# One maximum by GpSimd for all six stage 1 groups of batches 3 and 4

## The chip, the cores and the metric

The kernel runs on one core of one Trainium2 chip. The metric is the device time of one execution in microseconds (us). The core's engines run side by side, each through its own list of instructions in order: PE (TensorE, matmuls), DVE (VectorE), ACT (ScalarE), POOL (GpSimd) and SP (SyncE, which here only issues DMAs). They wait for each other through semaphores.

## What is computed

The input x has 4 batches of 12416 rows of 128 numbers. Two attention blocks follow each other, and a gated feed-forward layer:

```python
def mab(q, kv):
    s = scale * (q @ kv.transpose(0, 2, 1))
    s = s - s.max(-1, keepdims=True)
    a = np.exp(s)
    a /= a.sum(-1, keepdims=True) + 1e-09
    return a @ kv
h = mab(I, x)          # 32 learned rows look at all rows of a batch
attn = mab(x, h)       # every row of the batch looks at the 32 results

gate = 1.0 / (1.0 + np.exp(-(x @ w_gate)))    # x is attn here; d_ff is 1536
val = x @ w_val
out = (gate * val) @ w_out
```

Stage 1 is `h = mab(I, x)`: a softmax over all 12416 rows of a batch. Stage 2 is `mab(x, h)`: a softmax over 32 values in each row. The feed-forward layer takes nearly all of the time.

## The kernel before

**Steps and slots.** A batch's 97 chunks of 128 rows are six groups (0 to 5) of 16 chunks, and one chunk that is left over. The feed-forward layer works on blocks of four chunks, 24 blocks for a batch. A block takes eight steps, alternately of 1024 and 512 columns: PE fills a PSUM bank with gate values (`g_ps`) and one with values (`v_ps`), ACT takes tanh of the first (L1127), DVE multiplies (L1159, the product), and PE projects the product through `w_out` (L1200, into `acc_ps`). At the end of a block ACT copies the result to SBUF (L1219) and SP sends it out. A gate bank is filled two steps ahead, and is free only when tanh has read it. Two steps are one slot. `o` is the slot at which the layer begins a batch: 0, 96, 192, 288. The plan is a table, `at(slot, make, late)`: what stands at a slot is emitted after its first step, or with `late` after its second, and each engine does its work in that order. From slot 304 on the steps have another form, which the change does not touch.

**Beside the layer.** While the layer works on a batch, stage 1 of the next batch and stage 2 of both run in the gaps. Slots below are counted from `o`, so that slot 29 is `o + 29`; with `o` = 96 that is stage 1 of batch 3, with `o` = 192 that of batch 4. A block's output copy (L1219) falls late in slots 0, 4, 8 and so on.

**Stage 1, two ways.** (a) `plan_stage1`, for groups 2 and 3: PE scores the group (L246, 128x512 in PSUM), DVE takes the maximum of each row (L258), ACT takes the exponential from PSUM with that maximum as bias (L271), a DMA on SP's queue transposes it (L295), PE sums (L306), and ACT keeps the sum (L321). (b) `plan_shared`, for groups 0, 1, 4, 5 and the left-over chunk (`one`): ACT copies the scores to SBUF (`keep`, L368), into columns of the present batch's `xT` that stage 2 has done with (`place`). POOL raises a common maximum over them (`lift`, L385 to L389: subtract, clamp, add, for each group but the first; the last also folds the columns 512 to 256 to 128 and takes in `one`). DVE takes the maximum of the 128 columns left (`low`, L399), POOL adds the negative maximum to the scores (`lower`, L413), ACT takes the exponential (`weigh`, L417; L377 for `one`), then DMA (`turn`), sums (`part`) and one copy for two groups (`hold`, L431). `plan_combine` joins the partial sums of a batch; it weighs `NSH` of them.

**Stage 2 on POOL.** `plan_stage2` for a group: PE scores, ACT copies (L646), POOL takes the maximum and subtracts it (`lower`, L656 to L663), ACT takes the exponential (L672), POOL adds up and inverts (L680 to L686, `total`; L463 and on) and spreads the weights (L702, `spread`), SP transposes (L713). In this stretch POOL's list reads, by slots: `total` -1, `spread` 1, stage 2 `lower` 6, lifts 7, 11 and 15, `total` 19, `spread` 21, `low`'s lowerings 23 (groups 0, `one`, 1), stage 2 `lower` 24, an x load (L94, for `o` = 96 alone) 24, lowerings 29 (groups 4, 5). ACT's exponentials of stage 1 stand at 7, 11 (way a), 26, 27, 30, 42 and 46 (way b).

Of the kernel before, what the change touches and what calls it, by code (L numbers as in the profile page):

```python
# [17 lines left out]
P = 128  # L18
# [8 lines left out]
def kernel(  # L27
# [17 lines left out]
    NLO = NCH - NG * GC  # L45
# [10 lines left out]
    bp = ctx.enter_context(tc.tile_pool(name="bp", bufs=2))  # L56
    s1p = ctx.enter_context(tc.tile_pool(name="s1p", bufs=4))
# [26 lines left out]
    xn, xT = {}, {}  # L84
# [44 lines left out]
    for c, e in ((0, half0), (half0, n0)):  # L129
# [9 lines left out]
        out=identf[:],  # L139
        in_=identf[:],  # L140
# [42 lines left out]
    NS = len(groups)  # L183
    arrival = [0, NG] + list(range(1, NG))
    at_col = {s: p for p, s in enumerate(arrival)}
    EARLY = NS - 3
    SHARED = [(), (0, 1)] + [(0, 1, 4, 5)] * (B - 2)
    own = [[s for s in (arrival if b == 0 else [2, 3, 4, 5]) if s not in SHARED[b]] for b in range(B)]
    col_of = [{s: p for p, s in enumerate(o)} for o in own]
    PER = [1, 1] + [2] * (B - 2)  # L190
    NSH = [len(own[b]) + len(SHARED[b]) // PER[b] for b in range(B)]
    nml = const.tile([P, 1 + NS - EARLY], F32, tag="nml")
    l1l = const.tile([P, 1 + NS - EARLY], F32, tag="l1l")
    nm1s = [const.tile([P, NS], F32, name=f"nm1_{q}", tag=f"nm1_{q}") for q in range(2)]
# [28 lines left out]
    def at(slot, make, late=False):  # L223
        plan.setdefault((slot, late), []).append(make)


    def s1_place(b, s):
        return col_of[b][s]

# [8 lines left out]
        ng = min(4, n)  # L238
        return ng, n // ng, 32 * ng

    def s1_score_pe(b, s, tag):
        c0, n = groups[s]
        ng, w, R = s1_dims(s)
        s1 = ps.tile([P, 512], F32, tag=tag, name="s1_ps")
        for g in range(ng):
            nc.tensor.matmul(  # L246
                s1[32 * g : 32 * g + 32, 0 : w * P],
                indT[:],
                xT[b][:, c0 + g * w : c0 + (g + 1) * w, :].rearrange("c j t -> c (j t)"),
                start=True,  # L250
                stop=True,
            )
        return s1
# [39 lines left out]
    def s1_turn_dma(b, s, a1T):  # L293
        a1 = s1p.tile([P, 4, P], F16, tag="a1")
        nc.sync.dma_start(a1[:], a1T[:], transpose=True)  # L295
        return a1

    def s1_sum_pe(b, s, a1, hp, k0, k1, first=True, last=True):
        c0, n = groups[s]
        ng, w, R = s1_dims(s)  # L300
        for k in range(k0, min(k1, w)):
            for cols, src in ((slice(0, C), None), (slice(C, C + 1), ones16[:])):
                for g in range(ng):
                    if b == 0 and src is not None:
# [50 lines left out]
    def plan_shared(b, o, takes, tops, least, weighs, sums, holds, one, with_one):  # L355
        st = {}
        nm, hst, ns, no = nm1s[b % 2], hsts[b % 2], NSH[b], len(own[b])
        per = PER[b]

        def place(i):  # L360
            c = NLO + 8 * i
            return xT[b - 1][:, c : c + 8, :].rearrange("p j t -> p (j t)").bitcast(F32)

        def score(i):
            st["s1"] = s1_score_pe(b, SHARED[b][i], "m")

        def keep(i):
            nc.scalar.copy(out=place(i), in_=st["s1"][:])  # L368

        def score_one():  # L370
            s1 = s1_score_pe(b, NG, "m")
            st["one"] = s1p.tile([P, 512], F16, tag="a1T", name="one").bitcast(F32)[0:m, 0:P]
            nc.scalar.copy(out=st["one"], in_=s1[0:m, 0:P])

        def weigh_one():
            st["a1T"] = s1p.tile([P, 512], F16, tag="a1T", name="a1T")
            nc.scalar.activation(out=st["a1T"][0:m, 0:P], in_=st["one"], func=AF.Exp)  # L377

        def turn_one():
            st["a1"] = s1p.tile([P, 4, P], F16, tag="a1", name="a1")  # L380
            nc.sync.dma_start(st["a1"][:, 0, 0:m], st["a1T"][0:m, 0:P], transpose=True)

        def rise(near, far, w, R=P):
            top, r = place(4)[0:R, 0:w], place(5)[0:R, 0:w]
            nc.gpsimd.tensor_tensor(out=r, in0=far, in1=near, op=ALU.subtract)  # L385
            nc.gpsimd.tensor_scalar(
                out=r, in0=r, scalar1=BIG, scalar2=0.0, op0=ALU.min, op1=ALU.max
            )
            nc.gpsimd.tensor_tensor(out=top, in0=near, in1=r, op=ALU.add)  # L389

        def lift(i):
            rise(place(0) if i == 1 else place(4), place(i), 512)
            if i == len(SHARED[b]) - 1:
                for w in (256, 128):
                    rise(place(4)[:, 0:w], place(4)[:, w : 2 * w], w)
                rise(place(4)[0:m, 0:P], st["one"], P, m)

        def low():
            nc.vector.tensor_reduce(  # L399
                out=nm[:, no : no + 1],  # L400
                in_=place(4)[:, 0:128],
                axis=AX.X,
                op=ALU.max,
                negate=True,
            )
            lower(place(0), st["one"], place(1))
            for k in range(no + 1, ns):
                nc.gpsimd.tensor_copy(out=nm[:, k : k + 1], in_=nm[:, no : no + 1])

        def lower(*parts):  # L410
            for far in parts:
                near = nm[0 : far.shape[0], no : no + 1].to_broadcast(far.shape)
                nc.gpsimd.tensor_tensor(out=far, in0=far, in1=near, op=ALU.add)  # L413

        def weigh(i):
            st["a1T"] = s1p.tile([P, 512], F16, tag="a1T", name="a1T")
            nc.scalar.activation(out=st["a1T"][:], in_=place(i), func=AF.Exp)  # L417

        def turn(i):
            st[i] = s1_turn_dma(b, SHARED[b][i], st["a1T"])  # L420

        def part(i, k0, k1):
            if i % per == 0 and k0 == 0:
                st["hp"] = ps.tile([P, C + 1], F32, tag="m", name="hp_ps")
            if i == with_one and k0:
                s1_sum_pe(b, NG, st["a1"], st["hp"], 0, 1, False, False)
            s1_sum_pe(b, SHARED[b][i], st[i], st["hp"], k0, k1, i % per == 0, (i + 1) % per == 0)

        def hold(k):
            summed[b] += 1  # L430
            nc.scalar.copy(out=hst[:, no + k, :], in_=st["hp"][:])  # L431

        for i in range(len(SHARED[b])):
            at(o + takes[i], lambda i=i: score(i))
            at(o + takes[i], lambda i=i: keep(i), late=True)
            at(o + weighs[i], lambda i=i: weigh(i), late=True)
            at(o + weighs[i] + 1, lambda i=i: turn(i))
            at(o + sums[i], lambda i=i: part(i, 0, 2))
            at(o + sums[i] + 1, lambda i=i: part(i, 2, 4))
# [365 lines left out]
    a1T, a1 = {}, {}  # L805
# [46 lines left out]
    for j0, tag, copy in ((GC // 2, "v2", nc.scalar.copy), (GC - BC, "g1", nc.vector.tensor_copy)):  # L852
# [26 lines left out]
        out=top[:],  # L879
# [352 lines left out]
    for b in range(B):  # L1232
# [147 lines left out]
```

## Time and profile before

| what | value |
|---|---|
| three runs | 710.03, 710.17, 710.19 us; median 710.17 |
| the profiled execution | 710.04 us; its span, from first to last instruction, 708.3 us |
| DMA, mean over the span | 93 GB/s |
| products (L1159) of 1024 and of 512 columns, mean of one | 1.215 and 0.680 us |

The page gives each engine's busy time; the trace can be asked for instructions in order of time, for groups of them by line and shape, and for each engine's busy time in a stretch. Where instructions of one engine follow each other without a gap, the next one starts a little before the one ahead has ended, so that what an instruction costs its engine is read from start to start.

### The profile page before, as it was taken

How to read it: one execution, taken by the hardware profiler on the slowest of the kernel's cores; microseconds unless marked ns; L12 is line 12 of the kernel's file. 1: busy time of each engine (PE TensorE's matmuls, PEld its weight loads, DVE VectorE, ACT ScalarE, POOL GpSimd, SP SyncE). 2: the span in 40 equal slices, each digit the busy share in tenths (PEclk: the TensorE clock that was granted, in tenths of full speed). 3: DMA queues.
4: the chain of work that ended last, by engine and by line, in shares of the span. 5: the costliest groups of instructions: out<-in, count | busy, mean ns of one | idle time of the engine just before them, and what ended most of it. 6: DMA issues, size and time to landing. Idle time of an engine off the chain costs nothing.

```text
span 708.3 us, 21692 instructions
## 1 busy us (share of the span) xinstructions
PE 651.7 (92%) x8482; PEld 389.9 (55%) x8482; DVE 692.8 (98%) x806; ACT 680.2 (96%) x1115; POOL 458.3 (65%) x797
## 2 busy tenths in 40 slices
PE   7999899998999999999998989999899999999997
PEld 4555465555555555655555555555555555554555
DVE  4899999999999999999999999999999999999998
ACT  6799999999999999999999999999999999999997
POOL 4468865877558978668656896587757375482400
PEclk9999999999999999999999999999999999999999
DMA  9969854364583174156475141320322131221211
GB/s 214 181 123 192 139 133 93 76 121 86 114 161 80 57 127 101 51 125 118 92 139 124 54 77 53 69 76 31 78 63 74 47 60 48 59 76 46 63 46 46
DMA packets 118247, 65.80 MB, mean 93 GB/s; under 512 B 100320, under 2 KB 103296, under 8 KB 118144
## 3 DMA queue, kind: packets, MB, share of 16 engines
q1 hardware_dynamic: 113680, 50.93, 32.0%
q0 software_dynamic: 4272, 13.34, 10.7%
q8 instruction: 66, 1.08, 0.6%
q14 instruction: 37, 0.30, 0.2%
q10 hardware_dynamic: 192, 0.15, 0.1%
HBM read 27.80 MB, written 25.43 MB: 75 GB/s over the span
## 4 chain that ended last, share of the span: by engine, by line
DVE 35%; PE 29%; ACT 17%; issue 16%; DMA 2%; DVEq 0%; POOL 0%; POOLq 0%; ACTq 0%
DVE u L1159 33%; PE acc_ps L1200 14%; ACT t L1127 10%; PE v_ps L1064 10%; ACT xn L1106 5%; PE g_ps L1064 3%; DMA xn<-in_x_dram 2%; PE hp_ps L306 1%; ACT o L1219 1%; DVE nm L258 1%; DVEq L1159 0%; POOL xn L94 0%; ACT a1T L271 0%; ACT e L672 0%; ACT hwt L493 0%
## 5 line engine op out<-in xcount | busy, mean ns | idle before, releaser
L1159 DVE SCALAR_TENSOR_TENSOR u<-t,v_ps 128x512 f16<-128x512 f16 x609 | 528.3, 946 | 0.3 <-ACT t L1127 0.3
L1127 ACT ACTIVATE t<-g_ps 128x512 f16<-128x512 f32 x609 | 464.8, 821 | 10.5 <-ACT t L1127 4.0
L1200 PE MATMUL acc_ps<-wo,u 128*128 128x128 f16 x4644 | 333.8, 220 | 4.5 <-ACT o L1219 2.7
L1200 PEld LDWEIGHTS <-u 128*128 128x128 f16 x4644 | 261.9, 98 | 120.4 <-issue 117.8
L1064 PE MATMUL v_ps<-a2r,hwt 32*128 32x512 f16 (+1 forms) x1194 | 279.1, 372 | 40.5 <-DVE u L1159 39.1
L1064 PE MATMUL g_ps<-a2r,hwt 32*128 32x512 f16 (+1 forms) x1188 | 300.9, 376 | 1.0
L1064 PEld LDWEIGHTS <-hwt 32*128 32x128 f16 x2432 | 88.0, 91 | 150.8 <-issue 100.5
L1159 DVE SCALAR_TENSOR_TENSOR u<-xn,v_ps 128x1024 f16<-128x1024 f16 (+2 forms) x127 | 141.4, 1191 | 0.1
L1106 ACT ACTIVATE xn<-g_ps 128x512 f16<-128x512 f32 x249 | 126.7, 613 | 0.4
L702 POOL TENSOR_TENSOR a2n<-e,rs 128x2048 f16<-128x2048 f16 (+3 forms) x25 | 86.8, 3474 | 6.1 <-ACT t L1127 2.2
L680 POOL TENSOR_TENSOR sum<-e 128x256 f32<-128x256 f16 (+1 forms) x23 | 15.4, 670 | 109.7 <-ACT e L672 109.7
L463 POOL TENSOR_TENSOR near<-sme,minus 128x16 f32<-128x16 f32 (+1 forms) x22 | 65.2, 2965 | 1.6
L1219 ACT ACTIVATE o<-acc_ps 128x512 f32<-128x512 f32 x96 | 58.2, 606 | 0.9
L657 POOL TENSOR_SCALAR rise<-rise 128x256 f32<-128x256 f32 (+6 forms) x110 | 30.1, 273 | 9.6
L660 POOL TENSOR_TENSOR top<-top,rise 128x128 f32<-128x128 f32 (+3 forms) x88 | 28.3, 322 | 7.3
L680 POOL TENSOR_TENSOR sum<-sum 128x128 f32<-128x128 f32 (+3 forms) x92 | 28.3, 307 | 7.2
L656 POOL TENSOR_TENSOR rise<-top 128x128 f32<-128x128 f32 (+3 forms) x88 | 27.2, 309 | 6.9
L656 POOL TENSOR_TENSOR rise<-sc 128x256 f32<-128x256 f32 (+1 forms) x18 | 13.3, 738 | 21.0 <-ACT sc L646 20.9
L663 POOL TENSOR_TENSOR sc<-sc,top 128x512 f32<-128x512 f32 (+1 forms) x18 | 19.5, 1084 | 1.4
L612 PEld LDWEIGHTS <-xT 128*128 128x128 f16 x388 | 13.1, 96 | 11.7 <-issue 11.3
L94 POOL DMA_DIRECT2D xn<-in_x_dram x24 | 14.4, 607 | 6.5 <-DMA xn<-in_x_dram 5.6
L612 PE MATMUL s_ps<-hT,xT 128*128 128x32 f16 x388 | 18.1, 178 | 0.1
(173 smaller groups left out, 339.4 us busy)
## 6 DMA issues: line engine op xcount, KB each, us to landing
out_dram<-o SPq DMA_DIRECT2D x90, 256.0 KB, 2.2
xn<-in_x_dram POOLq DMA_DIRECT2D x19, 512.0 KB, 7.2
out_dram<-o SPq DMA_DIRECT2D x13, 128.0 KB, 1.7
xn<-in_x_dram POOLq DMA_DIRECT2D x3, 544.0 KB, 6.3
xT<-in_x_dram SPq DMA_DIRECT2D x1, 576.0 KB, 4.1
xT<-in_x_dram SPq DMA_DIRECT2D x1, 512.0 KB, 4.8
a2r<-a2n SPq DMA_TRANSPOSE x29, 4.4
xT<-xn SPq DMA_TRANSPOSE x27, 4.3
```

What stands on the lines that cost most here:

```text
L463: nc.gpsimd.tensor_tensor(out=near, in0=x, in1=minus, op=ALU.pow)
L612: nc.tensor.matmul(s2[:, j, :], xT[b][:, c + j, :], hT16[b][:], start=(j == 0), stop=whole and j == j1 - 1, skip_group_check=True,)
L656: nc.gpsimd.tensor_tensor(out=r, in0=far, in1=near, op=ALU.subtract)
L657: nc.gpsimd.tensor_scalar(out=r, in0=r, scalar1=BIG, scalar2=0.0, op0=ALU.min, op1=ALU.max)
L680: nc.gpsimd.tensor_tensor(out=d[:, 0:n, :], in0=src[:, :, 0:w], in1=src[:, :, w : 2 * w], op=ALU.add)
L702: eng.tensor_tensor(out=a2n[:, 0:n, :, :], in0=e.unsqueeze(2).to_broadcast((P, n, 4, m)), in1=rs.unsqueeze(2).unsqueeze(3).to_broadcast((P ...
L1064: st[what + "end"] = nc.tensor.matmul(to, hw[b][r : r + 32, j // 2, :], a2r[r : r + 32, o : o + nb, :].rearrange("p j t -> p (j t)"), star ...
L1106: nc.scalar.activation(out=ring_t(i, 1), in_=singles[i]["g"][:], func=AF.Tanh, scale=0.5)
L1127: st["tanh"] = nc.scalar.activation(out=st["t"][:, :, c:e], in_=st["g"][:, :, c:e], func=AF.Tanh, scale=0.5)
L1159: u = nc.vector.scalar_tensor_tensor(out=u16[:, :, c:e], in0=t16[:, :, c:e], scalar=1.0, in1=v32[:, :, c:e], op0=ALU.add, op1=ALU.mult,)
L1200: nc.tensor.matmul(acc[0][:, i, :], st["u"][:, n, ts(i, P)] if k < 2 else st["u1"][:, ts(i - st["kept"], P)], wo16[:, NI * (e % 2) + e // ...
L1219: nc.scalar.mul(out=o32[:], in_=acc[0][:], mul=0.5)
```

## The change

For batches 3 and 4 way (a) is dropped and all six groups go by way (b). The order among them is 2, 0, 3, 1, 4, 5. Groups 2 and 3 are scored and copied in two halves of 256 columns, and their exponentials are taken in four quarters of 128. Their scores lie in two tiles that are idle then (`"h"`, the other batch's `hst`, and `"x"`, the tile of `hx`); the common maximum and its scratch move to `home(2)` and `home(3)`. The partial sums are two instead of four.

By slots, before and after: copies -6, 2, 10, 14 become -7 and 1 (group 3, halves), -6 (0), -3 and -1 (group 2, halves), 2 (1), 10 (4), 14 (5); lifts 7, 11, 15 become 0, 2, 4, 11, 15; `low` 23 becomes 21 and lowers groups 0, `one`, 1; the later lowerings move from 29 (groups 4, 5) to 27 (groups 2, 3, 4, 5); exponentials become 26 (0), 29, 31, 33, 35 (group 2, quarters), 30 (1), 37, 39, 39, 41 (group 3, quarters), 42 (4), 46 (5); first sums become 31 (0), 33 (1), 40 (2), 44 (3), 48 (4), 51 (5); holds 45, 53 become 35, 53. The transposes of x of groups 2 and 3 move from -3 and 2 to -9 and -13. Stage 2's entries stay.

```diff
-    SHARED = [(), (0, 1)] + [(0, 1, 4, 5)] * (B - 2)
+    SHARED = [(), (0, 1)] + [(2, 0, 3, 1, 4, 5)] * (B - 2)
...
-    PER = [1, 1] + [2] * (B - 2)
-    NSH = [len(own[b]) + len(SHARED[b]) // PER[b] for b in range(B)]
+    SUMS = [(), ((0,), (1,))] + [((1, 3), (0, 2, 4, 5))] * (B - 2)
+    NSH = [len(own[b]) + len(SUMS[b]) for b in range(B)]
...
+    def at_half(time, make):
+        at(int(time // 1), make, late=time % 1 > 0)
...
+        homes = ('h', 0, 'x', 1, 4, 5) if b > 1 else (0, 1)
+        TOP, RISE = (2, 3) if b > 1 else (4, 5)
...
-        def keep(i):
-            nc.scalar.copy(out=place(i), in_=st["s1"][:])
+        def keep(i, part=slice(0, 4)):
+            cols = slice(part.start * P, part.stop * P)
+            nc.scalar.copy(out=place(i)[:, cols], in_=st["s1"][:, cols])
...
         def lift(i):
-            rise(place(0) if i == 1 else place(4), place(i), 512)
+            rise(place(0) if i == 1 else home(TOP), place(i), 512)
...
-            lower(place(0), st["one"], place(1))
+            soon = (1, 3) if b > 1 else (0, 1)
+            lower(place(soon[0]), st["one"], place(soon[1]))
...
-        def weigh(i):
-            st["a1T"] = s1p.tile([P, 512], F16, tag="a1T", name="a1T")
-            nc.scalar.activation(out=st["a1T"][:], in_=place(i), func=AF.Exp)
+        def weigh(i, part=slice(0, 4)):
+            cols = slice(part.start * P, part.stop * P)
+            if part.start == 0:
+                st["a1T", i] = s1p.tile([P, 512], F16, tag="a1T", name="a1T")
+            nc.scalar.activation(
+                out=st["a1T", i][:, cols], in_=place(i)[:, cols], func=AF.Exp
+            )
...
+        lowers = ((27, (0, 2, 4, 5)),) if b > 1 else ()
...
         at(o + least, low)
-        if len(SHARED[b]) > 2:
-            at(o + least + 6, lambda: lower(*[place(i) for i in range(2, len(SHARED[b]))]))
+        for slot, which in lowers:
+            at(o + slot, lambda which=which: lower(*[place(i) for i in which]))
...
-            parts = {2: (7, (16, 17, 17)), 3: (11, (18, 19, 19))}
-            turns = (-14, -5, -3, 2, 0, 8)
+            parts = {}
+            turns = (-14, -5, -9, -13, 0, 8)
             shared = (
-                (-6, 2, 10, 14),
-                (7, 11, 15),
-                23,
-                (26, 30, 42, 46),
-                (40, 42, 49, 51),
-                (45, 53),
+                ((-3, -1), (-6,), (-7.5, 0.5), (2,), (10,), (14,)),
+                (0, 2, 4, 11, 15),
+                21,
+                ((29, 31, 33, 35), (26,), (37, 38.5, 39, 41), (30,), (42,), (46,)),
+                (40, 31, 44, 33, 48, 51),
+                (35, 53),
                 (9, 27),
-                3,
+                5,
             )
```

In `lowers` and `soon` the numbers are places in the order above: 0 is group 2, 1 is group 0, 2 is group 3, 3 is group 1.

More of the change, by code (lines that the diff above doesn't have):

```diff
@@ L239, in s1_dims, with s1_score_pe @@
         return ng, n // ng, 32 * ng
-    def s1_score_pe(b, s, tag):
+    def s1_score_pe(b, s, tag, part=slice(0, 4)):
         c0, n = groups[s]
@@ L246, in s1_score_pe @@
             nc.tensor.matmul(
-                s1[32 * g : 32 * g + 32, 0 : w * P],
+                s1[32 * g : 32 * g + 32, part.start * P : min(part.stop, w) * P],
                 indT[:],
-                xT[b][:, c0 + g * w : c0 + (g + 1) * w, :].rearrange("c j t -> c (j t)"),
+                xT[b][:, c0 + g * w + part.start : c0 + g * w + min(part.stop, w), :].rearrange(
+                    "c j t -> c (j t)"
+                ),
                 start=True,
@@ L357, in plan_shared, with home, score @@
         nm, hst, ns, no = nm1s[b % 2], hsts[b % 2], NSH[b], len(own[b])
-        per = PER[b]
+        firsts, lasts = [g[0] for g in SUMS[b]], [g[-1] for g in SUMS[b]]
+        homes = ('h', 0, 'x', 1, 4, 5) if b > 1 else (0, 1)
+        TOP, RISE = (2, 3) if b > 1 else (4, 5)
         def place(i):
-            c = NLO + 8 * i
-            return xT[b - 1][:, c : c + 8, :].rearrange("p j t -> p (j t)").bitcast(F32)
-        def score(i):
-            st["s1"] = s1_score_pe(b, SHARED[b][i], "m")
-        def keep(i):
-            nc.scalar.copy(out=place(i), in_=st["s1"][:])
+            if homes[i] == "h":
+                return hsts[1 - b % 2].rearrange("p s c -> p (s c)")[:, 0:512]
+            if homes[i] == "x":
+                if "x" not in st:
+                    st["x"] = bp.tile([P, NS, C + 1], F32, tag="hx", name="far", bufs=1)
+                return st["x"].rearrange("p s c -> p (s c)")[:, 0:512]
+            return home(homes[i])
+        def home(k):
+            c = NLO + 8 * k
+            return xT[b - 1][:, c : c + 8, :].rearrange("p j t -> p (j t)").bitcast(F32)
+        def score(i, part=slice(0, 4)):
+            st["s1"] = s1_score_pe(b, SHARED[b][i], "m", part)
+        def keep(i, part=slice(0, 4)):
+            cols = slice(part.start * P, part.stop * P)
+            nc.scalar.copy(out=place(i)[:, cols], in_=st["s1"][:, cols])
         def score_one():
@@ L383, in rise @@
         def rise(near, far, w, R=P):
-            top, r = place(4)[0:R, 0:w], place(5)[0:R, 0:w]
+            top, r = home(TOP)[0:R, 0:w], home(RISE)[0:R, 0:w]
             nc.gpsimd.tensor_tensor(out=r, in0=far, in1=near, op=ALU.subtract)
@@ L391, in lift @@
         def lift(i):
-            rise(place(0) if i == 1 else place(4), place(i), 512)
+            rise(place(0) if i == 1 else home(TOP), place(i), 512)
             if i == len(SHARED[b]) - 1:
                 for w in (256, 128):
-                    rise(place(4)[:, 0:w], place(4)[:, w : 2 * w], w)
-                rise(place(4)[0:m, 0:P], st["one"], P, m)
+                    rise(home(TOP)[:, 0:w], home(TOP)[:, w : 2 * w], w)
+                rise(home(TOP)[0:m, 0:P], st["one"], P, m)
         def low():
@@ L400, in low @@
                 out=nm[:, no : no + 1],
-                in_=place(4)[:, 0:128],
+                in_=home(TOP)[:, 0:128],
                 axis=AX.X,
@@ L413, in lower, with pieces, add @@
                 nc.gpsimd.tensor_tensor(out=far, in0=far, in1=near, op=ALU.add)
-        def weigh(i):
-            st["a1T"] = s1p.tile([P, 512], F16, tag="a1T", name="a1T")
-            nc.scalar.activation(out=st["a1T"][:], in_=place(i), func=AF.Exp)
-        def turn(i):
-            st[i] = s1_turn_dma(b, SHARED[b][i], st["a1T"])
-        def part(i, k0, k1):
-            if i % per == 0 and k0 == 0:
+        def weigh(i, part=slice(0, 4)):
[5 more added lines that the diff above has]
+            )
+        def turn(i):
+            st[i] = s1_turn_dma(b, SHARED[b][i], st["a1T", i])
+        def pieces(slots):
+            cut = 4 // len(slots)
+            return [(slot, slice(k * cut, k * cut + cut)) for k, slot in enumerate(slots)]
+        def add(i, k0, k1):
+            if i in firsts and k0 == 0:
                 st["hp"] = ps.tile([P, C + 1], F32, tag="m", name="hp_ps")
@@ L426, in part @@
                 s1_sum_pe(b, NG, st["a1"], st["hp"], 0, 1, False, False)
-            s1_sum_pe(b, SHARED[b][i], st[i], st["hp"], k0, k1, i % per == 0, (i + 1) % per == 0)
+            s1_sum_pe(b, SHARED[b][i], st[i], st["hp"], k0, k1, i in firsts, i in lasts)
         def hold(k):
@@ L431, in hold @@
             nc.scalar.copy(out=hst[:, no + k, :], in_=st["hp"][:])
+        lowers = ((27, (0, 2, 4, 5)),) if b > 1 else ()
         for i in range(len(SHARED[b])):
[L434 to L439, printed above, removed]
+            for slot, part in pieces(takes[i]):
+                at_half(o + slot, lambda i=i, part=part: score(i, part))
+                at_half(o + slot + 0.5, lambda i=i, part=part: keep(i, part))
+            for slot, part in pieces(weighs[i]):
+                at_half(o + slot + 0.5, lambda i=i, part=part: weigh(i, part))
+            at(o + int(slot) + 1, lambda i=i: turn(i))
+            at(o + sums[i], lambda i=i: add(i, 0, 2))
+            at(o + sums[i] + 1, lambda i=i: add(i, 2, 4))
         at(o + one[0], score_one)
@@ L1263 @@
             turns = (5, 7, 17, 19, 22, 25, 9)
-            shared = (10, 14), (15,), 20, (26, 30), (33, 42), (34, 43), (13, 25), 0
+            shared = ((10,), (14,)), (15,), 20, ((26,), (30,)), (33, 42), (34, 43), (13, 25), 0
         else:
-            parts = {2: (7, (16, 17, 17)), 3: (11, (18, 19, 19))}
-            turns = (-14, -5, -3, 2, 0, 8)
+            parts = {}
+            turns = (-14, -5, -9, -13, 0, 8)
             shared = (
-                (-6, 2, 10, 14),
-                (7, 11, 15),
-                23,
-                (26, 30, 42, 46),
-                (40, 42, 49, 51),
-                (45, 53),
+                ((-3, -1), (-6,), (-7.5, 0.5), (2,), (10,), (14,)),
[4 more added lines that the diff above has]
+                (35, 53),
                 (9, 27),
-                3,
+                5,
             )
```

## The prediction

> **What bounds the kernel now.** I read the page first, then the busy time by stretches where stage 1 of batch 3 runs (slot 0 is at 201 us), then the timelines of ACT, DVE and POOL there.
>
> ```profile
> PE 651.7 (92%) x8482; PEld 389.9 (55%) x8482; DVE 692.8 (98%) x806; ACT 680.2 (96%) x1115; POOL 458.3 (65%) x797
> ```
>
> ```profile
> 200.00:220.00 20.00, 18.30 (x233) 11.12 (x231) 20.00 (x24) 19.71 (x31) 14.51 (x25) 1.00 0.72 155
> 220.00:240.00 20.00, 19.14 (x297) 11.95 (x294) 20.00 (x24) 19.70 (x32) 17.29 (x25) 1.00 0.15 49
> 240.00:260.00 20.00, 17.61 (x209) 10.26 (x207) 20.00 (x25) 19.70 (x31) 17.43 (x29) 1.00 0.51 88
> ```
>
> In the second view the columns after the length are PE, PEld, DVE, ACT, POOL, clock. DVE never rests: it is the bound, and ACT is close behind. POOL's 65% on the page hides that it is at 87% from 220 on.
>
> ```profile
> 201.02 0.60 ACT L1219 ACTIVATE o<-acc_ps 128x512 f32<-128x512 f32 x1
> ...
> 207.95 0.60 ACT L1219 ACTIVATE o<-acc_ps 128x512 f32<-128x512 f32 x1
> ...
> 215.53 0.61 ACT L1219 ACTIVATE o<-acc_ps 128x512 f32<-128x512 f32 x1
> ```
>
> ```profile
> 212.84 0.69 DVE L258 TENSOR_REDUCE nm<-s_ps 128x1 f32<-128x512 f32 x1
> ...
> 213.44 3.54 DVE L1159 SCALAR_TENSOR_TENSOR u<-t,v_ps 128x512 f16<-128x512 f16 x4
> ```
>
> Output copies end blocks of four slots. A block without a row maximum takes 6.93 us (201.02 to 207.95), 1.73 a slot; the one with L258 takes 7.58. From its start to the next product L258 costs DVE 0.60.
>
> **What is removed.** Two L258 in each of two batches: 4 x 0.60 = 2.4 us of the bound, if nothing else is late. The rest of this part asks what is late.
>
> **POOL's list.** This is the timeline of POOL for batch 3, first instructions of each task.
>
> ```profile
> 198.26 0.67 POOL L680 TENSOR_TENSOR sum<-e 128x256 f32<-128x256 f16 x1 [6.23 <-ACT e L672]
> ...
> 200.91 2.93 POOL L463 TENSOR_TENSOR near<-sme,minus 128x16 f32<-128x16 f32 x1
> ...
> 204.81 3.61 POOL L702 TENSOR_TENSOR a2n<-e,rs 128x2048 f16<-128x2048 f16 x1
> 212.08 0.73 POOL L656 TENSOR_TENSOR rise<-sc 128x256 f32<-128x256 f32 x1 [3.66 <-ACT sc L646]
> ...
> 219.71 1.27 POOL L385 TENSOR_TENSOR xT<-xT 128x512 f32<-128x512 f32 x1
> ...
> 223.10 1.27 POOL L385 TENSOR_TENSOR xT<-xT 128x512 f32<-128x512 f32 x1
> ...
> 227.32 1.27 POOL L385 TENSOR_TENSOR xT<-xT 128x512 f32<-128x512 f32 x1 [0.89 <-ACT xT L368]
> ...
> 235.59 0.65 POOL L680 TENSOR_TENSOR sum<-e 128x256 f32<-128x256 f16 x1
> ...
> 245.69 1.04 POOL L413 TENSOR_TENSOR xT<-xT,nm 128x512 f32<-128x512 f32 x1
> ...
> 248.18 0.72 POOL L656 TENSOR_TENSOR rise<-sc 128x256 f32<-128x256 f32 x1
> ...
> 255.77 0.67 POOL L94 DMA_DIRECT2D xn<-in_x_dram  x1
> 256.46 2.04 POOL L413 TENSOR_TENSOR xT<-xT,nm 128x512 f32<-128x512 f32 x2
> ```
>
> Start to start: `total` 2.65; `spread` 7.5 (200.91 to the end of L702, 208.42); stage 2 `lower` 7.63, later 7.59; a lift 3.39; the last lift with its folds 8.27; `total` and `spread` again 10.10; `low`'s lowerings 2.49; the load's issue 0.69; a lowering 1.02. The idle stretches are 3.66 and 0.89.
>
> After the change two lifts stand before stage 2's `lower`, one of them behind `total` and the others behind `spread`. That is five lifts for three, 2 x 3.39 = 6.78, and the idle time that they can fill is 4.55: POOL is 2.2 us later from there on, and has no rest. The list from 198.26: `total` to 200.91, lift 204.30, `spread` 211.8, two lifts 218.6, `lower` 226.2, lift 229.6, last lift 237.9, `total` and `spread` 248.0. Group 0 is lowered at 249.0, the others of `low` at 250.5. Then comes stage 2's `lower` of slot 24, to 258.1, the load to 258.8, and only then, from slot 27, group 2's lowering: **259.8**.
>
> **Who waits.** The timeline of ACT around slots 26 to 30:
>
> ```profile
> 247.58 0.63 ACT L417 ACTIVATE a1T<-xT 128x512 f16<-128x512 f32 x1
> 248.10 1.03 ACT L1127 ACTIVATE t<-g_ps 128x1024 f16<-128x1024 f32 x1
> 249.00 0.29 ACT L377 ACTIVATE a1T<-one 32x128 f16<-32x128 f32 x1
> 249.20 1.96 ACT L1127 ACTIVATE t<-g_ps 128x512 f16<-128x512 f32 x3
> 251.06 0.60 ACT L1219 ACTIVATE o<-acc_ps 128x512 f32<-128x512 f32 x1
> 251.53 3.09 ACT L1127 ACTIVATE t<-g_ps 128x1024 f16<-128x1024 f32 x4
> 254.51 0.63 ACT L417 ACTIVATE a1T<-xT 128x512 f16<-128x512 f32 x1
> ```
>
> ```profile
> 241.90 0.28 DVE L399 TENSOR_REDUCE nm<-xT 128x1 f32<-128x128 f32 x1
> ```
>
> Three waits appear, each a tighter form of the same lateness. (1) `low` moves from slot 23 (241.90) to 21: 241.9 - 3.46 - 1.2 = 237.2, but the folds end at 237.9, so DVE stands 0.7. (2) Group 0's exponential, slot 26, was at 247.58 and would be at 246.4 + 0.7 = 247.1; its lowering ends at 249.0: ACT stands 1.9. (3) Group 2's first quarter, late in slot 29: before, that place lies midway between 251.06 and 254.51, at 252.8. POOL is done at 259.8, **7.0 us after the old time**. Behind the waiting quarter on ACT stand the tanh's; behind them PE's gate fills and DVE's products. The third wait contains the other two and the 1.2 us gained, since after it the place in time is set by POOL alone.
>
> A quarter is not in the trace. Bounds: its nearest row, L377 of 32x128, takes 0.20 until tanh starts (249.00 to 249.20), and the full L417 takes 0.52; I take 0.20, and for DVE's distance behind ACT the same 0.2 (bounds 0 and 0.5), so they cancel.
>
> Batch 4 has the same list, from 366.03, without the load.
>
> ```profile
> 366.03 0.67 POOL L680 TENSOR_TENSOR sum<-e 128x256 f32<-128x256 f16 x1 [6.24 <-ACT e L672]
> ```
>
> ```profile
> 418.93 0.60 ACT L1219 ACTIVATE o<-acc_ps 128x512 f32<-128x512 f32 x1
> 419.40 3.10 ACT L1127 ACTIVATE t<-g_ps 128x1024 f16<-128x1024 f32 x4
> 422.38 0.63 ACT L417 ACTIVATE a1T<-xT 128x512 f16<-128x512 f32 x1
> ```
>
> Group 2 is lowered 61.5 - 0.7 = 60.8 after 366.03, at 426.9; slot 29 was at 420.7: **6.2 us**.
>
> **ACT's own load.** Four tanh take 2.76 (248.10 to 251.06, less 0.20), so two slots of 3.46 leave 0.70. Late in slots 37 to 41 lie four quarters and two copies of 0.47 (251.06 to 251.53): 1.74 for 1.40 of room. I take 0.2 a batch; bounds 0 (DVE's distance hides it) and 0.6, with quarters nearer to the full one. The half copies lie before slot 2, and what they cost is swallowed by wait 3. The two holds that go save ACT time where DVE is the bound: nothing. Scores in halves are more PE instructions before wait 3: nothing.
>
> The Trainium skill, "ScalarE: Activation LUTs", section "Rules for kernel authors", budgets about 0.3 us for an activation and 0.83 ns an element, an estimate of 0.41 for a quarter. By that the load term would be some 1 us a batch in place of 0.2; the row of L377 speaks for the smaller one.
>
> **SP and DMAs.** The transposes of x move to slots at which stage 1 still needs them 5 slots later or more: nothing. The distance from an exponential to its sum falls to 2.5 slots, 4.3 us, for group 1 (30 to 33) and group 3 (41 to 44).
>
> ```profile
> DMA to landing us min/median/max: 2.4/2.8/8.6
> ```
>
> That is L295, issue to landing. Exponential 0.6 and median 2.8 give 3.4: hidden, with under 1 us to spare. In batch 3 the loads of x, issued at 258.1 and after the lowerings at 262.9, lie around group 1's transpose; I take 0.6 there (bounds 0, and 8.6 + 0.6 - 4.3 = 4.9) and 0 in batch 4.
>
> **The sum.** 7.0 + 6.2 + 2 x 0.2 + 0.6 = 14.2 us on the profiled execution's 710.04: **724.2**. (The median, 710.17, is 0.13 above that execution.) A measurement of this kernel can tell about 0.2%, 1.4 us, from no change.
>
> **Rivals.** *The clock falls.* In wait 3 ACT stands from 254.4 (252.8 and the 1.6 of wait 2 over the old time) to 259.8, and PE, once its filled banks are full, for about 4.5 us of that. The trace shows one such rest, the end:
>
> ```profile
> 703.82 0.90 PE L1200 MATMUL acc_ps<-wo,u 128*128 128x128 f16 x13 [0.28 <-POOL u L1345]
> ```
>
> ```profile
> 704.00:709.00 5.00, 0.72 (x13) 0.54 (x10) 0.75 (x2) 0.38 (x1) 0.00 (x0) 0.95 0.15 52
> ```
>
> PE's last matmul ends near 704.7, and the granted clock, 1.00 in every stretch before, has 0.95 there: a fall some 4 us into the rest. PE at 92% of full speed cannot keep up at less. If the slow clock lasts as long as the rest, 4.5 us, half of it is lost: 2.2 a batch, 728.6 if both fall, 726.4 if one does. Chance 0.25: the rests are only a little longer than the one that showed the fall. The Trainium skill, "TensorE: Matmul & The Clock Gate", Part 1, has half speed after an idle window of about 3.4 us, and back after a busy one; by that 1.7 a fall, 727.6 for both. The trace agrees with the fall, and no run here shows the way back.
>
> *Only wait 2 bites.* If POOL takes the four lowerings ahead of the `lower` of slot 24, group 2 is done at 251.5 and wait 3 is gone; group 0's lowering at 249.0 against 247.58 still costs 1.4 a batch: 713.3 with ACT's load. Against it: POOL's rows follow the slots without exception (L656 of slot 24 before L413 of slot 29). Chance 0.05.
>
> *Faster: POOL is quicker than its rows.* The place is again slot 29, old time less the gain, 252.8 - 1.2 = 251.6. If POOL's 61.5 us from 198.26 took 53.3 or less, nothing would wait, and 2.4 less ACT's 0.4 remain: 708.0. It could be if POOL runs faster while DVE rests. Against it: POOL's L413 takes 1.04 and a lift 3.39 with DVE at 20.00 of 20, and DVE rests only after most of the chain has run. Chance 0.03.
>
> **How the numbers follow.** Forecast (both batches wait for POOL in slot 29, clock full): 0.67, 721.5 to 727 by the bounds of quarter, distance, load and transposes. Clock rival 0.25, up to 728.6; wait 2 alone 0.05; faster 0.03. The range 721 to 728.8 leaves out the last two and the ends of the others. Faster by over 0.2%: 0.03; within 0.2%: 0.02, from between the last two rivals; slower: 0.95.
>
> **What would show it.** Right: POOL without a rest from the `total` of slot -1 to the lowering of group 5; ACT's longest waits on POOL's L413 (its line will have moved), about 5.4 and 4.8 us at slot 29 and about 1.9 at slot 26; DVE idle by about 8 us in each of two stretches where it had none; no wait for stage 2's weights. Wrong: no such waits at a full DVE (then POOL's list isn't in the order that I read), PE's waits for transposes at slots 33 and 44 above 2 us, or a granted clock under 1.00 behind the waits (the rival).

## The result, and the profile after

| | median (lowest to highest), us | ratio to before, 95% interval |
|---|---|---|
| before, five runs | 710.05 (710.03 to 710.19) | |
| changed, five runs | 730.62 (730.03 to 732.06) | 1.0294 [1.0279, 1.0309] |
| forecast | 724.2 (721.0 to 728.8) | |

The change costs 20.6 us, 6.4 more than the 14.2 that were forecast. The execution profiled below took 732.06 us, the longest of the five.

The page of the changed kernel, its busy times and two of its rows in 40 slices:

```profile
PE 663.9 (91%) x8498; PEld 395.9 (54%) x8498; DVE 693.5 (95%) x802; ACT 683.4 (94%) x1131; POOL 472.6 (65%) x809
...
DVE  5899999999999859999999987999999999999998
...
PEclk9999999999999969999999998999999999999999
```

DVE has as much work as before (693.5 for 692.8 us) in a span that is 22 us longer: it waits. It does so in two places, slices 14 and 15 and slices 24 and 25, and right there the granted clock, which was full throughout before, falls.

The view of waits of the changed kernel says for what (waiting line, releaser, us in total, times, longest). ACT's exponentials (L417 before, now L437) wait for POOL's lowerings (L413, now L431):

```profile
ACT a1T L437 <- POOL hst L431: 9.2, 2, 4.7
...
ACT a1T L437 <- POOL xT L431: 3.7, 2, 1.9
```

```profile
DVE u L1188 <- PE g_ps L1093: 16.3, 15, 4.2
DVE u L1188 <- PE v_ps L1093: 3.8, 2, 1.9
```

ACT's waits are the forecast's wait 3 (`hst`, group 2) and wait 2 (`xT`, group 0), each once a batch. DVE, two steps behind, waits 20.1 us in all for PE's banks that come late for it; it had 15.5 us without work in the whole of before, and has 36.8 now.

POOL's timeline of the changed kernel around slot 27 of batch 3 (start, length):

```profile
198.56 0.67 POOL L709 TENSOR_TENSOR sum<-e 128x256 f32<-128x256 f16 x1 [6.54 <-ACT e L701]
...
248.09 1.04 POOL L431 TENSOR_TENSOR xT<-xT,nm 128x512 f32<-128x512 f32 x1
...
250.57 0.72 POOL L685 TENSOR_TENSOR rise<-sc 128x256 f32<-128x256 f32 x1
...
258.18 0.67 POOL L94 DMA_DIRECT2D xn<-in_x_dram  x1
258.88 1.05 POOL L431 TENSOR_TENSOR hst<-hst,nm 128x512 f32<-128x512 f32 x1
```

This is the list as it was read from the rows of before: `total` first (0.30 later than in before), group 0 lowered at 249.1 (forecast 249.0), then stage 2's `lower`, the load, and group 2 done at 259.93 (forecast 259.8). What ACT and DVE make of it:

```profile
249.16 0.63 ACT L437 ACTIVATE a1T<-xT 128x512 f16<-128x512 f32 x1 [1.87 <-POOL xT L431]
...
253.15 0.60 ACT L1248 ACTIVATE o<-acc_ps 128x512 f32<-128x512 f32 x1 [0.40 <-PE acc_ps L1229]
...
259.96 0.31 ACT L437 ACTIVATE a1T<-hst 128x128 f16<-128x128 f32 x1 [4.68 <-POOL hst L431]
260.17 1.50 ACT L1156 ACTIVATE t<-g_ps 128x1024 f16<-128x1024 f32 x2
...
267.01 0.60 ACT L1248 ACTIVATE o<-acc_ps 128x512 f32<-128x512 f32 x1 [0.72 <-PE acc_ps L1229]
```

```profile
238.03 0.29 DVE L416 TENSOR_REDUCE nm<-xT 128x1 f32<-128x128 f32 x1 [0.31 <-POOL xT L406]
...
251.18 1.82 DVE L1188 SCALAR_TENSOR_TENSOR u<-t,v_ps 128x1024 f16<-128x1024 f16 x2 [1.90 <-PE v_ps L1093]
...
261.87 1.22 DVE L1188 SCALAR_TENSOR_TENSOR u<-t,v_ps 128x1024 f16<-128x1024 f16 x1 [4.24 <-PE g_ps L1093]
```

All three waits are there: 0.31 for `low`, 1.87 for group 0, 4.68 for group 2. New are the two output copies (L1219, now L1248) that wait for PE, which no copy near these slots did before. Both fall in stretches of half clock. The granted clock in the records is constant over stretches of 3.41 us or whole multiples of it; cut at those places, the busy times of the changed kernel read (us, then PE, PEld, DVE, ACT, POOL busy, clock, DMA share, GB/s):

```profile
245.02:248.43 3.41, 3.01 (x39) 1.75 (x37) 3.41 (x5) 2.22 (x4) 3.41 (x2) 1.00 0.20 77
248.43:251.84 3.41, 1.51 (x15) 0.52 (x13) 1.51 (x3) 2.68 (x5) 3.26 (x6) 1.00 0.82 152
251.84:255.25 3.41, 3.41 (x30) 2.33 (x28) 2.70 (x4) 3.00 (x5) 2.81 (x7) 0.50 0.39 113
255.25:258.67 3.42, 1.89 (x23) 1.06 (x21) 2.10 (x3) 0.02 (x1) 2.92 (x8) 1.00 0.04 13
258.67:262.08 3.41, 0.85 (x18) 0.37 (x17) 0.21 (x1) 2.12 (x5) 3.38 (x5) 0.50 0.72 115
262.08:265.49 3.41, 3.41 (x44) 1.78 (x36) 2.37 (x3) 2.41 (x5) 1.36 (x2) 0.50 0.80 121
265.49:268.91 3.42, 3.02 (x38) 1.76 (x37) 2.28 (x3) 2.42 (x4) 0.00 (x0) 0.50 0.75 169
268.91:272.32 3.41, 3.41 (x41) 2.25 (x42) 2.12 (x3) 2.18 (x4) 0.00 (x0) 0.50 0.09 32
272.32:275.73 3.41, 3.07 (x46) 1.97 (x45) 2.93 (x4) 3.14 (x7) 2.19 (x7) 1.00 0.00 0
```

PE is busy for 1.51 of 3.41 us in the window of wait 2, and the next window runs at half clock; the same again after 1.89 of 3.42, at wait 3. The second fall lasts four windows, 13.65 us, though PE is busy for nearly all of the last three. In these DVE has 2.1 to 2.4 us of work in each 3.4: at half clock PE cannot feed it.

### The profile page after: what moved, and what is told of

It reads as the page before. It is cut to its first block, busy times and chain, and to the rows that moved or that the text cites. A ratio compares the mean times of both kernels' runs of the same rounds, so it can differ in the third digit from the quotient of the medians.

```text
span 730.3 us, 21759 instructions
## 1 busy us (share of the span) xinstructions
PE 663.9 (91%) x8498; PEld 395.9 (54%) x8498; DVE 693.5 (95%) x802; ACT 683.4 (94%) x1131; POOL 472.6 (65%) x809
## 4 chain that ended last, share of the span: by engine, by line
PE 29%; DVE 28%; issue 14%; ACT 13%; POOL 12%; DMA 4%; DVEq 0%; POOLq 0%; ACTq 0%
DVE u L1188 27%; PE acc_ps L1229 14%; PE v_ps L1093 9%; ACT t L1156 7%; ACT xn L1135 5%; PE g_ps L1093 3%; DMA xn<-in_x_dram 2%; POOL xT L406 2%; DMA a<-a1T 2%; POOL xT L402 1%; POOL top L689 1%; POOL rise L685 1%; ACT o L1248 1%; POOL a2n L731 1%; PE hp_ps L311 1%
## 5 line engine op out<-in xcount | busy, mean ns | idle before, releaser
L1229 PE MATMUL acc_ps<-wo,u 128*128 128x128 f16 x4644 | 338.6, 222 | 4.5 <-ACT o L1248 2.7
L1229 PEld LDWEIGHTS <-u 128*128 128x128 f16 x4644 | 266.6, 99 | 124.4 <-issue 121.2
L1093 PE MATMUL v_ps<-a2r,hwt 32*128 32x512 f16 (+1 forms) x1194 | 281.7, 376 | 39.7 <-DVE u L1188 36.8
L1248 ACT ACTIVATE o<-acc_ps 128x512 f32<-128x512 f32 x96 | 58.4, 608 | 3.0 <-PE acc_ps L1229 1.8
```

The costliest lines, as they stand in the source:

```text
L1093: st[what + "end"] = nc.tensor.matmul(to, hw[b][r : r + 32, j // 2, :], a2r[r : r + 32, o : o + nb, :].rearrange("p j t -> p (j t)"), star ...
L1229: nc.tensor.matmul(acc[0][:, i, :], st["u"][:, n, ts(i, P)] if k < 2 else st["u1"][:, ts(i - st["kept"], P)], wo16[:, NI * (e % 2) + e // ...
L1248: nc.scalar.mul(out=o32[:], in_=acc[0][:], mul=0.5)
```

## The experiments

Two theories stood against each other for the 6.4 us beyond the forecast. The first, A in the expectations, puts them down to the clock, which falls because PE rests in the waits. Its rivals put them down to ACT's additional pieces (halves and quarters) and to the transposes' shorter distance to their sums. A second question was whether POOL's lateness is the whole cause of the waits. The median of before, measured again beside these runs, was 709.88 (e1 to e4), 709.96 (e5 to e8) and 709.98 (e9, e10).

**e1_warm: PE kept busy in wait 3.** Added to the changed kernel are matmuls whose result nobody reads:

```diff
+        def warm(n):
+            w_ps = ps.tile([P, 512], F32, tag="m", name="warm_ps")
+            for _ in range(n):
+                nc.tensor.matmul(w_ps[:], wg16[:, 0:P], wg16[:, 0:512], start=True, stop=True)
+
+        if b:
+            at(o + 27, lambda: warm(8), late=True)
+            at(o + 30, lambda: warm(18), late=True)
```

> The changed kernel with matmuls that nobody reads (128x512, 8 late in slot 27 and 18 late in slot 30, batches 3 and 4), put where PE stands while ACT waits for POOL; everything else as it is. Theory A (the waits are POOL's lateness, 7.0 and 6.2 us, and what was lost behind them is PE's half clock): the waits of ACT stay as they are, the granted clock stays at 1.00, and some 4.3 us in batch 3 and 2.3 us in batch 4 come back: 724 us, 722.5 to 725. Rival B (behind the waits it is the late transposes and ACT's quarters that cost, and the clock only follows): the time stays near 730, within 1.5 us.

Measured: 730.57 us, 1.0284 [1.0268, 1.0300]. A's number missed and B's was met, but the cause that A names was not removed. The windows of this kernel's own clock stretches in batch 3:

```profile
255.95:259.36 3.41, 3.41 (x25) 1.85 (x24) 0.29 (x1) 0.00 (x0) 3.11 (x6) 1.00 0.09 13
259.36:262.77 3.41, 2.38 (x41) 1.36 (x39) 1.38 (x2) 3.08 (x6) 3.41 (x5) 1.00 0.91 157
262.77:266.18 3.41, 3.41 (x38) 1.77 (x35) 2.26 (x3) 2.62 (x6) 0.41 (x1) 0.50 0.82 124
```

PE still rested for 1.03 us at the end of the wait, and the clock still fell. In batch 4 wait 3 passed at full clock (slot 32 came only 6.3 us later), but then PE stood for the transposed exponentials of group 1 (1.03 us) and group 3 (1.46), and the clock fell behind the second. So the run settles nothing by its time. It led to e5, which closes these two holes, and to e6, its control.

**e5_warm_sums and e6_sums: the clock alone.** Both move the first sums of groups 1 and 3 a slot later, so that PE does not stand for the transposes; e5 keeps e1's matmuls too, with 23 in place of 18 for batch 3.

```diff
-                (40, 31, 44, 33, 48, 51),
+                (40, 31, 45, 34, 48, 51),
...
+            at(o + 27, lambda: warm(8), late=True)
+            at(o + 30, lambda b=b: warm(23 if b == 1 else 18), late=True)
```

> As e1_warm, with 23 matmuls in slot 30 of batch 3 (18 left 1.0 us of rest there, 18 in batch 4 none over 0.5), and the first sums of groups 1 and 3 one slot later (34 and 45 for 33 and 44), so that PE doesn't wait for their transposes. Theory A (7.0 and 6.2 us from POOL's list, some 0.5 a batch from ACT's load, the rest from the clock and from transposes): clock 1.00 throughout, 723.5 to 725.5. Rival B (something else costs the 6 us behind the waits): 728 or more with the clock at 1.00.

> The changed kernel with the first sums of groups 1 and 3 one slot later alone. PE's waits for transposes in it come to 1.6 us: if they are on the path and nothing hides them, 729.0; if the half clock is what PE stands on there and the transposes are hidden by it, 730.6, no change; theory A says between the two, 729 to 730.6, with the same falls of the clock.

Measured: e5 725.51 us, 1.0217 [1.0204, 1.0231]; e6 730.00, 1.0275 [1.0260, 1.0291]. Span and mean granted clock of the profiled executions, e5's and then e6's:

```profile
core 0: 723.4 us, clock 0.999
```

```profile
core 0: 728.2 us, clock 0.979
```

e5 does more work on PE than e6, waits as long for POOL (its longest wait of an exponential is even longer, 5.3 us), and is 4.5 us faster: that is the clock, for two batches, in each of which it fell twice in e6. It is A's forecast at its upper edge, where B had 728 or more. Output copies on ACT's timeline measure the rest. Of before, slots 32 and 48 of batch 3 and slot 32 of batch 4:

```profile
257.98 0.61 ACT L1219 ACTIVATE o<-acc_ps 128x512 f32<-128x512 f32 x1
...
285.68 0.60 ACT L1219 ACTIVATE o<-acc_ps 128x512 f32<-128x512 f32 x1
...
425.85 0.60 ACT L1219 ACTIVATE o<-acc_ps 128x512 f32<-128x512 f32 x1
```

Of e5, slots 32 to 48 of batch 3 and slot 32 of batch 4:

```profile
264.99 0.64 ACT L1248 ACTIVATE o<-acc_ps 128x512 f32<-128x512 f32 x1
272.10 0.69 ACT L1248 ACTIVATE o<-acc_ps 128x512 f32<-128x512 f32 x1
279.27 0.70 ACT L1248 ACTIVATE o<-acc_ps 128x512 f32<-128x512 f32 x1
286.33 0.60 ACT L1248 ACTIVATE o<-acc_ps 128x512 f32<-128x512 f32 x1
293.81 0.60 ACT L1248 ACTIVATE o<-acc_ps 128x512 f32<-128x512 f32 x1
...
440.41 0.63 ACT L1248 ACTIVATE o<-acc_ps 128x512 f32<-128x512 f32 x1
```

Slot 32 is 7.0 us late (264.99 for 257.98): POOL's wait of batch 3. At slot 48 it is 8.1 (293.81 for 285.68): 1.1 us came after the wait, in blocks of 7.1 to 7.5 us where before had 6.9. Slot 32 of batch 4 is 14.6 late (440.41 for 425.85): 6.4 more, POOL's wait of batch 4. So of e5's 15.5 us the waits are 13.4, and 2.1 are left for the pieces. Of these the copies show 1.1 and 0.6 (behind slot 32 of batch 4); 0.4 no copy shows, since the profiled executions lie only 15.2 us apart.

**e2_early and e3_both: POOL's list in time.** e2 lowers groups 2 and 3 together with groups 0 and 1, ahead of stage 2's `lower`. e3 also lets the copies of groups 2 and 3 trade places, so that the first lift goes to slot -3, into POOL's 6.5 us of rest ahead of `total`.

```diff
-            soon = (1, 3) if b > 1 else (0, 1)
-            lower(place(soon[0]), st["one"], place(soon[1]))
+            soon = (1, 3, 0, 2) if b > 1 else (0, 1)
+            lower(place(soon[0]), st["one"], *[place(i) for i in soon[1:]])
...
-        lowers = ((27, (0, 2, 4, 5)),) if b > 1 else ()
+        lowers = ((27, (4, 5)),) if b > 1 else ()
```

The second step, in e3 alone:

```diff
-            turns = (-14, -5, -9, -13, 0, 8)
+            turns = (-14, -5, -13, -9, 0, 8)
             shared = (
-                ((-3, -1), (-6,), (-7.5, 0.5), (2,), (10,), (14,)),
-                (0, 2, 4, 11, 15),
+                ((-7.5, -4.5), (-6,), (-1, 0.5), (2,), (10,), (14,)),
+                (-3, 2, 4, 11, 15),
```

> The changed kernel with groups 2 and 3 lowered together with 0, the left-over chunk and 1 in low (slot 21), ahead of stage 2's lower of slot 24; groups 4 and 5 stay at 27. Theory A (wait 3 is POOL's order): the wait at slot 29 goes, the wait at slot 26 stays at 1.9 us; each batch then stands 1.6 us behind the kernel before at slot 26 and loses up to 0.9 more to ACT's quarters: 713 to 715, up to 717 if the clock still falls at slot 26. Rival B (transposes and quarters cost the rest of the 20 us): no less than 720.

> As e2_early, and the copies of groups 2 and 3 trade places (group 2 in halves at slots -7 and -4, group 3 at -1 and 1; their transposes of x at -13 and -9), so that the first lift can stand at slot -3, in POOL's rest of 6.2 us ahead of total. Theory A: POOL's list is then 3.4 us earlier, no engine waits for it, and what is left is 2.4 us of row maxima gained, less what halves and quarters cost ACT, 0.3 to 1.5 us a batch: 708.3 to 710.6, middle 709.4. Rival B: 715 or more. If the maxima were not worth 2.4 us, above 711.

Measured: e2 718.66 us, 1.0123 [1.0109, 1.0137]; e3 711.60, 1.0024 [1.0015, 1.0033]. Both lie above what was expected: e2 above the 717 allowed for with a fall, though below the 720 of its rival, and e3 above 710.6. e2 is the prediction's rival "only wait 2 bites" made real, and is 5 us above the 713.3 priced there: one wait of 1.9 us a batch is left, and it lowers the clock by itself. Two windows of e2:

```profile
248.54:251.95 3.41, 1.53 (x15) 0.56 (x13) 1.53 (x3) 2.88 (x5) 3.41 (x5) 1.00 0.88 165
251.95:255.36 3.41, 3.41 (x32) 2.21 (x31) 2.77 (x4) 3.01 (x6) 3.07 (x7) 0.50 0.34 106
```

e3 has neither wait nor fall (clock 1.00 until the end) and is 7.1 us faster than e2. Of that 3.7 are ACT's waits for POOL and 0.5 DVE's (`low`); the other 2.9, some 3 us, are put down to two falls, of 3.41 us in batch 3 and 6.83 in batch 4. That is a difference of kernels whose copies also stand at other places. With POOL in time 19 of the 20.6 us are gone. What e3 still loses, 1.7 us, is neither a wait for POOL nor clock.

**e4_idle_lifts and e10_four_idle: POOL's lateness alone.** These go from the kernel before, with DVE's maxima where they were, and add lifts on an idle tile whose values nobody uses: two a batch in e4, four in e10.

```diff
+        def idle_lift(q):
+            scr = hsts[q].rearrange("p s c -> p (s c)")[:, 0:512]
+            nc.gpsimd.tensor_tensor(out=scr, in0=scr, in1=scr, op=ALU.subtract)
+            nc.gpsimd.tensor_scalar(
+                out=scr, in0=scr, scalar1=BIG, scalar2=0.0, op0=ALU.min, op1=ALU.max
+            )
+            nc.gpsimd.tensor_tensor(out=scr, in0=scr, in1=scr, op=ALU.add)
+
+        if b:
+            for slot in (0, 2):
+                at(o + slot, lambda q=b % 2: idle_lift(q))
```

In e10 the slots are `(0, 2, 3, 4)`.

> The kernel before, with two lifts more on POOL at slots 0 and 2 of batches 3 and 4, over a tile that is idle then and whose values nobody uses. Theory A: POOL is 2.2 us later at low's lowerings, group 0's exponential at slot 26 waits about 1.4 us in each batch, nothing else waits: 712.5 to 713, up to 715 if the clock falls there. Rival (POOL has room, the change was late for another reason): 710.0, no wait.

> The kernel before with four idle lifts (slots 0, 2, 3, 4) instead of e4_idle_lifts' two, which were 2.83 us each and moved POOL's list by 1.1. Theory A: 11.3 us of work into 4.55 of rest puts group 0's lowering 6.8 us later, ACT stands 5.9 us at slot 26 in each batch; with a PE that is idle for most of a 3.4 us window the clock falls, which cost 2.2 a batch in the changed kernel: 722 to 726, and half clock in the trace behind both waits though nothing of stage 1 was changed. Rival (the falls come of the changed kernel's own PE work): clock 1.00, 721.5 to 722.

Measured: e4 710.58 us, 1.0009 [1.0000, 1.0019]; e10 725.50, 1.0219 [1.0205, 1.0233]. e4's expectation missed on its price for a lift. POOL's timeline of e4:

```profile
200.68 1.04 POOL L1282 TENSOR_TENSOR hst<-hst 128x512 f32<-128x512 f32 x1
201.80 0.61 POOL L1283 TENSOR_SCALAR hst<-hst 128x512 f32<-128x512 f32 x1
202.50 1.04 POOL L1286 TENSOR_TENSOR hst<-hst 128x512 f32<-128x512 f32 x1
```

With the same tile for both operands a pass takes 1.04 us, for 1.27 with two tiles, and the lift 2.8 for 3.39. Two of them fill 5.7 us, POOL's idle 4.55 takes most, and the 1.1 left is about the reserve that POOL had ahead of ACT (0.85: in before group 0's lowering ended at 246.73, and ACT took it up at 247.58). The one wait of ACT for it that the view of waits lists in e4 is 0.2 us, and the clock does not fall. So e4 shows how little POOL had to spare, and e10 what follows beyond it. ACT in e10 and the clock around it:

```profile
253.68 0.63 ACT L417 ACTIVATE a1T<-xT 128x512 f16<-128x512 f32 x1 [5.32 <-POOL xT L413]
```

```profile
249.50:252.91 3.41, 0.71 (x9) 0.31 (x7) 0.86 (x2) 0.00 (x0) 3.41 (x2) 1.00 0.02 5
252.91:256.32 3.41, 0.99 (x4) 0.10 (x3) 0.40 (x1) 2.56 (x5) 3.31 (x6) 0.50 0.81 149
256.32:259.74 3.42, 3.42 (x28) 2.25 (x28) 2.65 (x4) 2.94 (x5) 2.80 (x7) 0.50 0.31 80
```

The waits for POOL in e10, ACT's and those of DVE, whose maximum in `low` (L399) now comes late too:

```profile
ACT a1T L417 <- POOL xT L413: 10.5, 2, 5.3
```

```profile
DVE nm L399 <- POOL xT L389: 1.3, 2, 0.7
```

Together they are 11.8 us, and the run is 15.5 slower than before: 3.7 us for two falls, with not one half, quarter or moved transpose in the kernel. That is inside A's range, while the rival at full clock had 722 at most. So the falls need nothing of the changed kernel but POOL's lateness.

**e7_both_sums, e8_whole, e9_spread: what the pieces cost.** e7 is e3 with the sums of e6. e8 is e7 with the exponentials of groups 2 and 3 whole, at slots 29 and 39. e9 is e7 with the pieces spread: group 2's second half is copied half a slot earlier, late in slot -5 instead of early in -4, group 3's quarters stand two slots apart, and its sum follows group 4's.

```diff
-                ((29, 31, 33, 35), (26,), (37, 38.5, 39, 41), (30,), (42,), (46,)),
+                ((29,), (26,), (39,), (30,), (42,), (46,)),
```

The lines of e9 against e7:

```diff
-                at_half(o + slot, lambda i=i, part=part: score(i, part))
+                late = 0.5 if slot == -5 else 0
+                at_half(o + slot + late, lambda i=i, part=part: score(i, part))
...
-                ((-7.5, -4.5), (-6,), (-1, 0.5), (2,), (10,), (14,)),
+                ((-7.5, -5), (-6,), (-1, 0.5), (2,), (10,), (14,)),
...
-                ((29, 31, 33, 35), (26,), (37, 38.5, 39, 41), (30,), (42,), (46,)),
-                (40, 31, 45, 34, 48, 51),
+                ((29, 31, 33, 35), (26,), (37, 39, 41, 43), (30,), (42,), (46,)),
+                (40, 31, 48, 34, 45, 51),
```

> e3_both with the first sums of groups 1 and 3 one slot later. In e3_both PE waited 0.6 us in each batch for group 3's transpose at slot 44, where the output copies fell back by 0.7: theory A gives 711.6 - 1.2 = 710.4. Rival (it is ACT's quarters alone that make those 0.7): 711.6.

> e7_both_sums with the exponentials of groups 2 and 3 whole (slots 29 and 39) in place of four quarters each. A whole one costs ACT 0.52 to the next start and four quarters 0.80; if ACT's total decides, 0.28 a group less: 709.5 to 710.0. If what decides is how much one instruction pushes back the tanh behind it (0.2 us of distance), each whole one costs DVE 0.3 and the quarters nothing: 711 to 711.6.

> e7_both_sums with ACT's small pieces spread over the odd slots: group 2's second half copied late in slot -5 instead of early in -4 (where its output copies fell back by 0.5 to 0.8 us in a batch), group 3's quarters late in 37, 39, 41, 43 instead of 37, 39, 39, 41, and its sum at 48 behind group 4's at 45. Theory A (what is left is ACT's pieces where two of them meet in one slot): 0.4 and 0.3 us a batch back, 709.0 to 709.6. Rival (each piece costs its own time wherever it stands): 710.4.

Measured: e7 710.37 us, 1.0006 [0.9997, 1.0014]; e8 710.49, 1.0007 [0.9998, 1.0016]; e9 709.31, 0.9991 [0.9982, 1.0000]. Later sums are worth 1.2 us once nothing else is late (e3 to e7). e8 came out between its two expectations and decides for neither: quarters and whole exponentials cost the same here. e9 gains 1.1 us over e7 by places alone; by the output copies 0.8 of it come ahead of slot 0, where the half copy moved, and 0.3 between slots 32 and 48, where the quarters moved. It is the best of the kernels that were run, and at 0.1% under before it lies at the edge of what can be told. In e7's trace the blocks that hold the quarters are long; output copies of slots 28 to 44 of batch 3:

```profile
250.56 0.59 ACT L1248 ACTIVATE o<-acc_ps 128x512 f32<-128x512 f32 x1
...
257.51 0.65 ACT L1248 ACTIVATE o<-acc_ps 128x512 f32<-128x512 f32 x1
...
264.64 0.69 ACT L1248 ACTIVATE o<-acc_ps 128x512 f32<-128x512 f32 x1
...
271.81 0.69 ACT L1248 ACTIVATE o<-acc_ps 128x512 f32<-128x512 f32 x1
...
278.87 0.60 ACT L1248 ACTIVATE o<-acc_ps 128x512 f32<-128x512 f32 x1
```

6.95, 7.13, 7.17 and 7.06 us, for 6.92 in before: 0.6 a batch.

## Why the prediction was wrong

**The step that failed is the clock.** The forecast, at 0.67, had "clock full", and the rival in which it falls got 0.25, because "the rests are only a little longer than the one that showed the fall". From one fall, some 4 us into the rest at the end of before, a rest of about 4 us was read as the condition, and wait 2 was left out of the question altogether. The runs show another condition: PE busy for 0.57 or less of one 3.41 us window (once 0.70). A rest of 1.6 us did it (wait 2 in e2), and once one of 1.03 (e1). By that both batches had to fall, and at both waits. The wait of 0.2 us in e4 brought none. The rival's price, 2.2 a batch or 4.4, came near what was measured, 4.5 between e5 and e6 and 3.7 in e10, but by luck: it reckoned one fall a batch that lasts as long as PE's rest, 4.5 us, while the changed kernel's trace has two falls a batch, of 3.41 and 13.65 us in batch 3. Nor is the clock alone the whole miss: 4.5 on top of 724.2 is 728.7, and most of the rest is ACT's load, below.

The Trainium skill, "TensorE: Matmul & The Clock Gate", Part 1, has the window, 3.4 us, and half speed. The trace agrees with both (3.41 and 0.50). It speaks of an idle window, and here windows with 0.21 to 0.57 of PE's time busy (0.70 once, e1) were enough; it has full speed back after at least one busy window: the fall at 251.84 ended after one, while that at 258.67 outlasted one in which PE was busy throughout, at 262.08.

The terms against the runs, in us for both batches:

| term | forecast | measured | from |
|---|---|---|---|
| waits for POOL | 13.2 | 13.4 | slot 32 in e5: 7.0 and 6.4 |
| ACT's load | 0.4 | 2.1 | e5 less its waits |
| transposes | 0.6 | 0.6 | changed kernel less e6; e6's runs spread over 1.8, so not shown |
| clock | 0 | 4.5 | e6 less e5 |
| sum | 14.2 | 20.6 | |

Three of the four measured rows are differences between runs in a chain, so that their sum comes to 20.6 whatever the causes are; what speaks for the causes is the single steps: e5 and e6 differ only in the matmuls that nobody reads, e6 and the changed kernel only in the places of two sums.

**POOL's list: right**, its end to 0.13 us and its length to 0.2 (61.4 for 61.5). The three waits stood where they were put; wait 1 was 0.3 for 0.7, wait 2 1.87 for 1.9. Wait 3 measured 4.7 and 4.5 for 5.4 and 4.8 because the half clock had delayed ACT before it got there: in e5, at full clock, it was 5.3 and 4.6. It was also right that wait 3 contains the other two waits and the gain.

**What was removed: right, and worth nothing.** Two maxima of 0.60 a batch gave 1.3 us before slot 12 (output copies there stood 0.8 us early, from 0.5 late at slot 4), and wait 3 swallowed them. In e9, without a wait and with the pieces well placed, some 0.7 us of the 2.4 remain, at the edge of what can be told.

**ACT's load: mis-sized.** The price of a quarter was right (259.96 to 260.17 is 0.21, and 0.20 was taken), the sum of work against room was not: 0.2 a batch for 1.1 and 0.6 in e5 after the waits. Room was counted over several slots together, while the runs answer to where each piece stands: e9 has the pieces of e7 at other places and is 1.1 us faster. That a piece delays the product of its own step, which DVE cannot make good, would explain it, but no run tried that alone. The Trainium skill's estimate from "ScalarE: Activation LUTs", "Rules for kernel authors", came to about 1 us a batch: nearer in the sum, by a price for a quarter (0.41) that is twice the measured one.

**Transposes.** PE's waits for them were the predicted small ones, 1.6 us in all, none over 0.6; in e3, with nothing late ahead of them, moving their sums gave 1.2 us.

Open: what decides when the clock comes back (after 3.41, 6.83, 10.24 or 13.65 us at half), and why a window at 0.70 busy brought a fall in batch 3 of e1, while one at 0.70 in its batch 4 and windows at 0.67 and 0.70 in e10 brought none.

## What to carry to other kernels

An engine at 65% of the span can be full where the work is added: write out its list for that stretch, start to start, and the time at which its result is ready comes out to some tenths of a microsecond. Then ask what PE does in that wait: a rest of 1.6 us was followed by some 1.5 us lost to the clock here (e2 against e3), so a helper that is only just late can cost much more than the wait. Where POOL must take work from DVE, give it the work where it rests (the lift at slot -3 of e3), and try other places for each added piece of ACT: e9 gained 1.1 us by that.

## What the runs showed of the hardware

- The granted clock changes only at places 3.41 us apart, and to 0.50 at once. Every fall ahead of the end, over all these runs, followed a window in which PE was busy for 0.21 to 0.57 of it, but for one in e1 that followed 0.70. After the first 20 us no window at full clock with PE busy for less than 0.67 passed without a fall.
- Matmuls that nobody reads hold the clock: e5 has 57 more matmuls than e6, a mean granted clock of 0.999 for 0.979, and is 4.5 us faster.
- POOL's TENSOR_TENSOR of 128x512 f32 takes 1.27 us with two different tiles, 1.04 with the same tile twice (e4), as with a column for the second operand (L413 in before).
